# Batches 0 and 1 of a fused attention and swish-gate kernel in new orders on all engines

## Chip, cores and metric

The kernel runs on one core of one Trainium2 chip. The metric is the device time of one execution in microseconds (us). Most executions agree within 0.3%; for the comparisons below each kernel was run several times, in turn with the kernel before on the same chip. A profile is one execution with the hardware profiler; its span is about 1.8 us shorter than the device time. Times inside a profile count from the start of that span.

The engines are called TensorE (PE in the profile, PEld for its weight loads), VectorE (DVE), ScalarE (ACT), GpSimd (POOL) and the SyncE queue (SP), which issues the DMAs.

## The reference, cut to what matters

```python
# q, k, v: 8 batches x 8 heads x 576 x 64, float32
q_s = softmax(q, axis=-1); k_s = softmax(k, axis=2)
kv  = einsum('bhsd,bhse->bhde', k_s, v)
x   = einsum('bhsd,bhde->bhse', q_s, kv)      # -> 4608 tokens x 512
h   = x @ w_in                                # 512 x 2048
g   = h * sigmoid(beta * h)
out = g @ w_out                               # 2048 x 512
```

The main work is two large products, h and the output. One batch (512 of its 576 tokens; the tails form a ninth group) needs 16 h products of 4 matmuls and 16 output products of 4 matmuls, each matmul 128x128 by 128x512. Before the first h there is attention: exp(q), its sum and product, transposes, exp(k), kv, its norm, and x.

## The kernel before

The parts that the change touches (cuts are marked `# ...`):

```python
# exp(k) of batches 0 and 1: two heads share a tile, each in its own half of the
# partitions and of the columns; the other half is zero
def kz_exp(b, j, m=1):
    for e in range(2):
        r = slice(e * D, (e + 1) * D)
        nc.scalar.activation(ek[b][r, j : j + m, :, e * D : (e + 1) * D],
                             k_st[b][r, j : j + m, :].rearrange(...), ACTF.Exp)

def kv_mm(b, jj, n=2, tag="att"):             # batches 0 and 1: whole-array products
    # ...
    for i in range(RW):                       # RW = 9
        nc.tensor.matmul(t[:, jl, 0:D1], ek[b][:, j, i, :], va[b][:, j, i, :], ...)

# loads: q, k, v of batch 0, then w_in and w_out by turns
w_load("in", 0, 0); w_load("in", 0, 1); w_load("out", 0, 0); w_load("in", 1)
w_load("out", 0, 1); w_load("out", 1); w_load("in", 2); w_load("out", 2); w_load("in", 3)
# ... q, k, v of batch 1 among the last w_out

for p in range(HP):                           # batch 0: kv and x by head pair
    attn0(p)                                  # va cast, kv, norm
    # ...
    if p >= 1: x_mm(0, p - 1, nc.scalar)
    if p >= 2:
        for j in range(2): mm_a(0, j, [p - 2])   # first h, ahead of the last kv and x
# ...
for u in range(4, NJ):                        # then one h product, one output product
    mm_a(0, u); mm_b(0, u - LAG)              # ...
```

The softmax here doesn't subtract the row's maximum and nothing guards it: scores larger than these inputs give would overflow.

## Time and profile before

| | before |
|---|---|
| median of three runs | 288.42 us (288.05 to 288.63) |
| span of the profile | 286.1 us |
| TensorE busy | 278.1 us, 97% |
| first h matmul / dense stream of h and outputs | 16.08 us / 18.79 us |
| first output product of batch 1 | 52.61 us |

The first fence holds two lines of the page: busy time of each engine, and the shares of the chain of waits (the work that ended last, followed back through what released it).

```profile
PE 278.1 (97%) x1611; PEld 129.6 (45%) x1611; DVE 179.8 (63%) x281; ACT 162.7 (57%) x236; POOL 43.5 (15%) x58
...
PE 93%; DMA 4%; SPq 1%; POOL 0%; ACT 0%; DVE 0%; issue 0%
```

TensorE is the limit, and the chain runs over it nearly all the way. A matmul of 512 columns has a duration of 379 ns, but in a dense stretch the next one starts 0.216 us later; they overlap. So a busy share says little about gaps. The gaps in this document are taken from the starts: time from one start to the next, less 0.42 ns for each column (512 columns take 0.216 us in a dense stretch). A few matmul records are missing from the traces, and a gap of exactly 0.22 us is one of those.

The next fence is the timeline of the head: start, duration (from the first start to the last end of a merged run), engine, line, operation, out<-in, count, and in brackets the idle time before it and what ended it.

```profile
8.26 5.57 ACT L158 ACTIVATE ek<-k_st 64x576 bf16<-64x576 f32 x8 [1.16 <-DMA k_st<-in_k_dram]
...
14.98 1.04 POOL L145 CAST w_in_b<-w_in 128x1024 bf16<-128x1024 f32 x1 [0.81 <-DMA w_in<-in_moe_w_in_dram]
...
16.08 0.60 PE L358 MATMUL h<-xT,w_in_b 128*128 128x512 bf16 x2 [1.03 <-POOL w_in_b L145]
...
16.52 0.45 PE L264 MATMUL kv<-va,ek 128*128 128x65 bf16 x9
...
17.03 0.59 PE L358 MATMUL h<-xT,w_in_b 128*128 128x512 bf16 x2
...
17.73 0.39 PE L314 MATMUL x<-qsT,kvp 128*128 128x512 bf16 x1
...
17.96 0.59 PE L358 MATMUL h<-xT,w_in_b 128*128 128x512 bf16 x2
...
18.79 2.32 PE L358 MATMUL h<-xT,w_in_b 128*128 128x512 bf16 x10 [0.24 <-ACT xT L143]
```

The reader sees ScalarE making exp(k) in eight runs of 64 partitions, 0.68 us each; the first h waiting for its weights; and the last kv and x standing behind that h in TensorE's order. By 18.79 six h matmuls are done (the pairs at 16.08, 17.03 and 17.96; ten more follow, and the first four h products have sixteen), so the dense stream starts, in effect, at 18.79 - 6 x 0.216 = 17.49 us.

### The profile page before, as it was taken

To read this page: it belongs to the slowest core of one execution; us is meant where nothing else is said; L and a number is where in the kernel's file an instruction comes from. 1 tells how busy PE (TensorE), PEld (TensorE's weight loads), DVE (VectorE), ACT (ScalarE), POOL (GpSimd) and SP (SyncE) were. 2 spreads that over 40 slices of the span, in tenths; PEclk is the share of its full clock that TensorE was granted. 3 is DMA by queue.
4 is the path that set the end of the run, shared out by engine and by line. 5 is a ranking of instruction groups with operands and counts; after the bars stand their busy time and mean duration, and the time that the engine had idled before them with its cause. 6 is when DMAs were issued, how large, how long until landed. Compare 5 with 4: busy or idle time off the path is not lost.

```text
span 286.1 us, 4169 instructions
## 1 busy us (share of the span) xinstructions
PE 278.1 (97%) x1611; PEld 129.6 (45%) x1611; DVE 179.8 (63%) x281; ACT 162.7 (57%) x236; POOL 43.5 (15%) x58
## 2 busy tenths in 40 slices
PE   8789999999999999999999999999999999999995
PEld 2434445444444444444444444444445444445543
DVE  7935397695478456854694569546964596455361
ACT  4763596684486448735683468355934564554451
POOL 4358824200030021000300030002000000000000
PEclk9999999999999999999999999999999999999999
DMA  7999999908932973198219912794370033005003
GB/s 244 376 385 387 371 387 320 287 2 247 299 149 63 314 179 137 31 330 201 90 60 247 303 40 113 169 260 124 147 205 17 1 149 73 0 0 149 0 0 147
DMA packets 56371, 50.08 MB, mean 175 GB/s; under 512 B 26256, under 2 KB 48032, under 8 KB 56352
## 3 DMA queue, kind: packets, MB, share of 16 engines
q1 hardware_dynamic: 56208, 49.69, 56.5%
q8 instruction: 12, 0.20, 0.3%
q10 hardware_dynamic: 144, 0.13, 0.1%
q14 instruction: 7, 0.06, 0.1%
HBM read 36.71 MB, written 9.44 MB: 161 GB/s over the span
## 4 chain that ended last, share of the span: by engine, by line
PE 93%; DMA 4%; SPq 1%; POOL 0%; ACT 0%; DVE 0%; issue 0%
PE h L358 44%; PE acc L399 42%; DMA k_st<-in_k_dram 2%; PE x L314 2%; DMA w_in<-in_moe_w_in_dram 2%; PE kv L276 2%; PE acc L391 1%; PE kv L264 1%; PE tp L250 0%; POOL w_in_b L145 0%; SPq L85 0%; PE x L318 0%; ACT xT L143 0%; SPq L106 0%; DVE kvp L309 0%
## 5 line engine op out<-in xcount | busy, mean ns | idle before, releaser
L368 ACT ACTIVATE th<-h,beta_t 128x512 bf16<-128x512 f32 x144 | 98.5, 687 | 98.8 <-PE h L358 96.9
L370 DVE SCALAR_TENSOR_TENSOR g<-th,h 128x512 bf16<-128x512 bf16 x144 | 97.8, 681 | 88.8 <-ACT th L368 87.4
L358 PE MATMUL h<-xT,w_in_b 128*128 128x512 bf16 x576 | 145.3, 379 | 1.3 <-POOL w_in_b L145 1.0
L399 PE MATMUL acc<-w_out_b,g 128*128 128x512 bf16 x560 | 141.9, 379 | 0.0
L358 PEld LDWEIGHTS <-w_in_b 128*128 128x128 bf16 x576 | 55.4, 98 | 67.0 <-issue 2.7
L399 PEld LDWEIGHTS <-g 128*128 128x128 bf16 x560 | 54.5, 98 | 65.4 <-DVE g L370 0.5
L145 POOL CAST va<-v_st 128x2048 bf16<-128x2048 f32 (+2 forms) x12 | 16.9, 1414 | 146.6 <-DMA v_st<-in_v_dram 146.4
L225 DVE TENSOR_REDUCE rq<-eq 128x16 f32<-128x1024 bf16 x18 | 21.6, 1198 | 2.3 <-ACT eq L214 2.3
L231 DVE TENSOR_TENSOR eq<-eq,rq 128x1024 bf16<-128x1024 bf16 x18 | 22.1, 1229 | 0.1
L214 ACT ACTIVATE eq<-q_st 128x1024 bf16<-128x1024 f32 x16 | 16.3, 1047 | 3.0 <-DMA q_st<-in_q_dram 3.0
L143 ACT CAST xT<-x 128x512 bf16<-128x512 f32 x20 | 11.6, 586 | 10.8 <-PE x L314 10.0
L145 DVE COPY o<-acc 128x512 f32<-128x512 f32 (+1 forms) x19 | 12.1, 669 | 3.4 <-PE acc L399 3.2
L143 ACT COPY o<-acc 128x512 f32<-128x512 f32 (+1 forms) x18 | 9.5, 578 | 5.8 <-PE acc L399 2.9
L169 ACT ACTIVATE ek<-k_st 128x1024 bf16<-128x1024 f32 x12 | 12.6, 1047 | 0.0
L314 PE MATMUL x<-qsT,kvp 128*128 128x512 bf16 x32 | 11.7, 380 | 0.4 <-DVE kvp L309 0.2
L158 ACT ACTIVATE ek<-k_st 64x576 bf16<-64x576 f32 x16 | 10.9, 678 | 1.3 <-DMA k_st<-in_k_dram 1.2
L472 PE MATMUL warm<-kvp 128*128 128x512 bf16 x34 | 10.1, 439 | 1.2 <-DVE kvp L500 1.2
L145 DVE CAST xT<-x 128x512 bf16<-128x512 f32 x16 | 10.9, 683 | 0.5 <-PE x L314 0.5
L145 POOL CAST w_out_b<-w_out 128x1024 bf16<-128x1024 f32 x8 | 8.4, 1058 | 6.0 <-DMA w_out<-in_moe_w_out_dram 6.0
L309 DVE TENSOR_TENSOR kvp<-kv,rk 64x256 bf16<-64x256 f32 (+2 forms) x24 | 8.0, 334 | 0.6
L145 POOL CAST w_in_b<-w_in 128x1024 bf16<-128x1024 f32 x7 | 7.2, 1041 | 3.5 <-DMA w_in<-in_moe_w_in_dram 3.4
L472 PEld LDWEIGHTS <-kvp 128*128 128x128 bf16 x34 | 3.5, 109 | 5.4 <-issue 2.2
(40 smaller groups left out, 75.2 us busy)
## 6 DMA issues: line engine op xcount, KB each, us to landing
out_dram<-o SPq DMA_DIRECT2D x14, 512.0 KB, 3.4
q_st<-in_q_dram SPq DMA_DIRECT2D x6, 1024.0 KB, 6.4
k_st<-in_k_dram SPq DMA_DIRECT2D x6, 1024.0 KB, 9.4
v_st<-in_v_dram SPq DMA_DIRECT2D x6, 1024.0 KB, 10.7
w_in<-in_moe_w_in_dram SPq DMA_DIRECT2D x3, 1024.0 KB, 9.6
k_st<-in_k_dram SPq DMA_DIRECT2D x8, 288.0 KB, 8.1
q_st<-in_q_dram SPq DMA_DIRECT2D x4, 512.0 KB, 7.8
w_out<-in_moe_w_out_dram SPq DMA_DIRECT2D x4, 512.0 KB, 9.3
```

What stands on the lines that cost most here:

```text
L143: eng.copy(dst, src)
L145: eng.tensor_copy(dst, src)
L169: nc.scalar.activation(ek[b][:, :, h, :].rearrange("p i h d -> p h i d"), k_st[b][:, h, 0 : R * D].rearrange("p h (i d) -> p h i d", i=R), ...
L214: nc.scalar.activation(eq[b][:, :, s * m : (s + 1) * m, :].rearrange("p i h d -> p h i d"), q_st[b][:, s * m : (s + 1) * m, :].rearrange(" ...
L225: nc.vector.tensor_reduce(rq[b][:, 0, :, h], eq[b][:, :, h, :], axis=AX.X, op=ALU.add)
L231: nc.vector.tensor_tensor(eq[b][:, :, h, :], eq[b][:, :, h, :], rq[b][:, 1, :, h].unsqueeze(3).to_broadcast((P, R, m, D)), ALU.mult,)
L314: nc.tensor.matmul(t[:], kvp[:, c, j, :], qsT[c][:, :, j, :])
L358: nc.tensor.matmul(h[:], w_in_b[:, kt, ds(j * P, P)], x_of(c)[:, kt, :], start=(kt == 0), stop=(kt == KT - 1),)
L368: nc.scalar.activation(th[:], h[:], ACTF.Tanh, scale=beta_t[:, j : j + 1])
L370: nc.vector.scalar_tensor_tensor(out=g[:], in0=th[:], scalar=1.0, in1=h[:], op0=ALU.add, op1=ALU.mult)
L399: nc.tensor.matmul(acc[st][:], g[:, ds(st * P, P)], w_out_b[:, j, :], start=(j == 0), stop=(j == NJ - 1),)
L472: nc.tensor.matmul(t[:, 0:cols], kvp[:, B - 1, 0, :], kvp[:, B - 1, :, :].rearrange("p j r -> p (j r)")[:, 0:cols],)
```

## The change

The intent: have x ready when the first w_in piece arrives, run the first eight h products while w_out is still on its way, and give each engine an order of its own for batches 0 and 1. Everything from the fifth h product of batch 1 on is the same code, apart from the layout of the weights. The core of the diff (cut):

```diff
-        for e in range(2):                     # exp(k): dense, one activation per head pair
-            ... nc.scalar.activation(ek[b][r, j : j + m, :, e * D : (e + 1) * D], ...)
+        nc.scalar.activation(ek[b][:, j, :], k_st[b][:, j, :], ACTF.Exp)

+    def kvz_mm(b, j, tag="att"):               # kv in two quadrants of the array
+        for i in range(RW):
+            for e in range(2):
+                nc.tensor.matmul(att_of[b][r, j, 0:D1], ek[b][r, j, ds(i * D, D)], va[b][r, j, i, :],
+                                 ..., tile_position=(e * D, e * D))

-    w_out_d = moe_w_out.rearrange("(j p) f -> p j f", p=P)
+    w_out_d = moe_w_out.rearrange("(hh p e) f -> p hh e f", p=P, e=2)     # 4 KB runs, blocks 0, 1
+    w_out_4 = moe_w_out.rearrange("(blk p e) f -> p blk e f", p=P, e=4)   # 8 KB runs, blocks 2, 3

# so column q of an h product is every 2nd (blocks 0, 1) or every 4th column of w_in
+    w_in_u = [t[:].rearrange("p kt (q e) -> p kt e q", e=2) for t in w_in_b]
+            if blk >= EB:                      # blocks 2, 3: reordered by the cast
+                evac(eng, w_in_c[blk][:, c], t[:, c, :].rearrange("p kt (q e) -> p kt e q", e=4))

+    w_load("in", 0, 0)                         # all of w_in 0 and 1 ahead of w_out
+    ...beta_r, beta_q (behind w_in 0, 0)...
+    w_load("in", 0, 1); w_load("in", 1, 0); w_load("in", 1, 1)
+    w_load("out", 0, 0); w_load("out", 0, 1); w_load("in", 2); w_load("out", 1); w_load("in", 3)
+    ...
+    xpe(0, 2, "acc3"); ...; w_castk(0, 0, 1, G); beta_pe("acc1"); w_castk(0, 0, 0, A)
+    ...; xpe(0, 3, "acc2"); beta_ev()
+    hpe(0, 0, [0], "b0"); hpe(0, 1, [0], "b1"); ...      # h 0 to 7, then
+    mm_b(0, 0); mm_b(0, 1); mm_b(0, 2); mm_b(0, 3)       # outputs 0 to 3
+    hpe(0, 10, ...); hpe(0, 9, ...); hpe(0, 11, ...); hpe(0, 8, ...)
+    mm_b(0, 4) ... mm_b(0, 7); hpe(0, 12, ...) ... hpe(0, 15, ...); mm_b(0, 8) ...
+    # batch 1's kv in four groups (pairs 0, 3, 1, 2) among the outputs 9 to 14
```

## The prediction

> **What bounds it now.** TensorE: 97% busy on the page; the chain of waits puts 93% of the span on it. From 18.79 us its matmuls stand 0.216 us apart (timeline). So the time is the start of the dense h/output stream plus a fixed stream and tail. With four h matmuls already done, that start is effectively 18.79 - 0.86 = 17.9 us. Two things make it late (timeline): ScalarE runs eight 64-row exp(k) of 0.68 us, 8.26 to 13.83, before it evacuates any x; and TensorE, in order, takes the first h (16.08; its w_in landed at 14.93, GpSimd's cast took 1.04) ahead of the last kv/x pair, whose x is evacuated at 18.7. Second limit: DMA, 365 to 390 GB/s from 5 to 48 us; the last w_out lands at 41.4, batch 1's last v at 44.4.
>
> **What changes.**
> - Dense exp(k): four 128x576 activations for eight of 64x576; about 2.7 us less ScalarE per batch. The zero fills (1.98 us VectorE, 2.11 GpSimd) were off the path.
> - Loads: the same bytes precede the first w_in piece, so it should land at 14.9 again. Its cast is split over GpSimd and ScalarE (estimate 0.55 us). First h near 15.8, with x0 to x3 just ahead; w_in pieces at 1.47 us steps then feed h0 to h7 without w_out. Estimate: h6 ends at 22.7, minus 32 x 0.216 gives an effective start of 15.8: gain 2.1 us.
> - kv in quadrants: batches 2 to 7 already run pairs in about 32 ns, the full-array form takes 31: no gain. The Trainium skill (TensorEngine Tiling, Key Properties) says that a mode switch drains TensorE; this trace shows about 0.1 us at each edge of batch 2's group. Four groups in batch 1: about 0.8 us lost. Two warm matmuls fewer (0.43) and the small gaps pay that back.
> - Strided weights (every second w_in column for j below 8): the Trainium skill (TensorE: Matmul & The Clock Gate, weight-path perf modes) allows a column step in the fast load; loads take 98 ns under 216 ns matmuls.
> - w_out in 4 and 8 KB runs: 2 KB runs already reach about 387 GB/s; at most 0.3 us.
>
> **On the path.** By TensorE, batch 1's dense stream begins about 2.3 us earlier (effective 49.3 to 47.0). By DMA: loads end near 44.5 with the last w_out half, then cast 1.05, two output products 1.73, one x: about 47.1. The limits coincide, so slips add: w_in block 2 lands near 24.7, needed at 26.0; block 3 near 30, two strided GpSimd casts, needed at 33.0; w_out block 2 at 35.7, needed at 36.9. I allow 0.3 us. After batch 1's start the code is the same.
>
> **Predicted: 286.4 us** (8 in 10: 285.4 to 287.8). Faster by over 2%: 0.02; within 2%: 0.95; slower by over 2%: 0.03.
>
> **What would show it.** Right: first w_in still landing near 14.9, first h near 15.8, h6 ending near 22.7, batch 1's dense start 2 us earlier, the rest unchanged, 5 us less ScalarE in exp(k), kv pairs at about 32 ns. Wrong: first h after 16.5; TensorE gaps waiting for casts of w_in blocks 2, 3 or w_out 2, 3; DMA of batch 1 ending after 45.
>
> **What would make it wrong.** Strided weight loads that no longer hide (288 of them; 20 ns each would cost 5.8 us); strided GpSimd casts far above 1.04 us; lower GB/s with 1 KB runs; TensorE's clock dropping in an early gap.

## The result, and the profile after

| | before | after |
|---|---|---|
| median, first rounds | 288.40 us (4 runs) | 287.29 us (287.14 to 287.56, 4 runs) |
| ratio | | 0.9964, 95% interval 0.9947 to 0.9981 |
| median, repeated | 288.04 us (11 runs) | 287.59 us (286.94 to 287.88, 6 runs) |
| ratio, repeated | | 0.9978, 0.9964 to 0.9992 |
| span of the profile | 286.1 us | 285.8 us |
| first h / first output product | 16.08 / 20.95 us | 16.36 / 23.27 us |
| first output product of batch 1 | 52.61 us | 52.33 us |

A ratio is the mean time of one kernel's runs over that of the other's in the same rounds, so not quite the ratio of the medians. Executions over 1.5% slower than the fastest of the same kernel are left out of the means. By the medians the change gains 0.5 to 1.1 us, about a quarter to a half of the 2.0 us forecast. From the first output product of batch 1 to the end both profiles take the same (286.10 - 52.61 = 233.49, 285.78 - 52.33 = 233.45 us): all of the difference lies before it.

The same two lines of the page, after:

```profile
PE 277.2 (97%) x1655; PEld 130.2 (46%) x1684; DVE 178.0 (62%) x279; ACT 164.3 (57%) x238; POOL 42.9 (15%) x58
...
PE 85%; DMA 9%; DVE 1%; SPq 1%; ACT 1%; issue 1%; POOL 0%
```

The chain of this execution goes over DMA for 9% instead of 4%. Alone that proves little, as the share moves from trace to trace (2% and 12% for two versions below, 10% for one with the old order of loads). The timeline after, head first, then the two places where TensorE stops:

```profile
15.03 0.62 ACT L160 CAST w_in_b<-w_in 128x512 bf16<-128x512 f32 x1
15.06 0.62 POOL L162 CAST w_in_b<-w_in 128x512 bf16<-128x512 f32 x1 [0.82 <-DMA w_in<-in_moe_w_in_dram]
...
15.36 0.36 PE L577 MATMUL tb<-ident,beta_r 4*128 4x4 f32 x2
15.59 0.61 PE L579 MATMUL tb<-ident,beta_q 2*128 2x2 f32 x4
...
16.14 0.39 PE L370 MATMUL x<-qsT,kvp 128*128 128x512 bf16 x1
...
16.36 7.07 PE L420 MATMUL h<-xT,w_in_b 128*128 128x512 bf16 x31
...
25.26 2.06 ACT L160 CAST w_in_c<-w_in 128x1024 bf16<-128x1024 f32 x1 [0.44 <-DMA w_in<-in_moe_w_in_dram]
25.29 2.05 POOL L162 CAST w_in_c<-w_in 128x1024 bf16<-128x1024 f32 x1 [2.94 <-DMA w_in<-in_moe_w_in_dram]
...
27.39 3.63 PE L420 MATMUL h<-xT,w_in_c 128*128 128x512 bf16 x16 [0.51 <-POOL w_in_c L162]
...
30.60 4.04 POOL L162 CAST w_in_c<-w_in 128x1024 bf16<-128x1024 f32 x2 [1.68 <-DMA w_in<-in_moe_w_in_dram]
...
34.70 3.63 PE L420 MATMUL h<-xT,w_in_c 128*128 128x512 bf16 x16 [0.22 <-DVE rq L238]
```

Three things are to be seen. The h stream is dense from its first matmul, 16.36, against an effective 17.49 before: 1.13 us won. Both casts of w_in block 2 take 2.05 us where a cast of as many elements took 1.04 before, and the h of that block follows their end; the gap between matmul starts there is 0.67 us. Block 3's two casts take 4.04 us on GpSimd alone, end at 34.64, and the h follows at 34.70: the gap is 0.39 us. The profile names VectorE's `rq` as that releaser because it too ended just then; the h matmul reads nothing of it, so the cast is the one to take. The first h itself was ready to go earlier: its casts end at 15.68, but six tiny transposes of beta and the last x stand before it.

### The profile page after: what moved, and what is told of

It reads as the page before. It is cut to its first block, busy times and chain, and to the rows that moved or that the text cites. A ratio compares the mean times of both kernels' runs of the same rounds, so it can differ in the third digit from the quotient of the medians.

```text
span 285.8 us, 4292 instructions
## 1 busy us (share of the span) xinstructions
PE 277.2 (97%) x1655; PEld 130.2 (46%) x1684; DVE 178.0 (62%) x279; ACT 164.3 (57%) x238; POOL 42.9 (15%) x58
## 4 chain that ended last, share of the span: by engine, by line
PE 85%; DMA 9%; DVE 1%; SPq 1%; ACT 1%; issue 1%; POOL 0%
PE h L420 40%; PE acc L468 39%; DMA q_st<-in_q_dram 4%; DMA k_st<-in_k_dram 3%; DMA w_in<-in_moe_w_in_dram 3%; PE x L370 2%; PE kv L330 2%; PE acc L460 1%; SPq L115 1%; DVE g L434 1%; PE kv L289 1%; DVE rq L237 0%; POOL w_in_b L162 0%; ACT eq L226 0%; PE tp L274 0%
## 5 line engine op out<-in xcount | busy, mean ns | idle before, releaser
L468 PE MATMUL acc<-w_out_b,g 128*128 128x512 bf16 x547 | 138.9, 379 | 0.6 <-issue 0.2
L420 PE MATMUL h<-xT,w_in_c 128*128 128x512 bf16 x280 | 71.8, 379 | 1.1 <-POOL w_in_c L162 0.5
L420 PE MATMUL h<-xT,w_in_b 128*128 128x512 bf16 x281 | 70.9, 379 | 0.6
L420 PEld LDWEIGHTS <-w_in_b 128*128 128x128 bf16 x288 | 28.1, 98 | 33.9 <-issue 1.6
L420 PEld LDWEIGHTS <-w_in_c 128*128 128x128 bf16 x288 | 27.2, 98 | 32.6 <-POOL w_in_c L162 1.7
L162 POOL CAST va<-v_st 128x576 bf16<-128x576 f32 (+1 forms) x14 | 18.6, 1328 | 145.7 <-DMA v_st<-in_v_dram 145.6
L162 DVE CAST xT<-x 128x512 bf16<-128x512 f32 x19 | 13.0, 685 | 0.7 <-PE x L370 0.7
L162 POOL CAST w_in_c<-w_in 128x1024 bf16<-128x1024 f32 x3 | 6.1, 2047 | 4.6 <-DMA w_in<-in_moe_w_in_dram 4.6
L162 POOL CAST w_out_b<-w_out 128x1024 bf16<-128x1024 f32 x6 | 6.2, 1041 | 3.2 <-DMA w_out<-in_moe_w_out_dram 3.2
L174 ACT ACTIVATE ek<-k_st 128x576 bf16<-128x576 f32 x8 | 5.5, 681 | 2.0 <-DMA k_st<-in_k_dram 1.9
```

The source lines that it names most:

```text
L162: eng.tensor_copy(dst, src)
L420: nc.tensor.matmul(h[:], w_in_u[j // 2][:, kt, j % 2, :] if j < 4 * EB else w_in_c[j // 4][:, kt, j % 4, :], x_of(c)[:, kt, :], start=(kt ...
L468: nc.tensor.matmul(acc[st][:], g[:, ds(st * P, P)], w_out_b[:, j, :], start=(j == 0), stop=(j == NJ - 1),)
```

## Experiments

"The changed kernel" is the kernel after the change. The runs came in three groups of four (after_again to e12; e1b to e6; d1 to e17), each group on one chip with its own runs of the kernel before, so across groups the ratios are to be compared rather than the medians. The 95% intervals of a ratio are about +-0.0012 to 0.0023, that is 0.35 to 0.7 us. A trace is one execution and often not a typical one: those of e12 and e13 were the fastest of their six runs, those of e2, d1 and e17 the slowest.

### after_again: the changed kernel once more

> The changed kernel again, for a second trace and a tighter ratio. The two profiled runs differ by only 0.3 us in span (286.1 and 285.8), the medians by 1.1 us. If the trace pair tells the truth, the median gain is 0.3 to 0.6 us; if the profiled run of before was a lucky one, the gain stays near 1.1 us. In the trace I expect the same two TensorE stalls, 0.67 us near 27.4 us and 0.39 us near 34.7 us, and casts of w_in blocks 2 and 3 of 2.05 us each.

Measured: 287.59 us, ratio 0.9978 (0.9964 to 0.9992); span 285.9 us. The casts again took 2.02 to 2.05 us, and the stalls before blocks 2 and 3 were 0.87 and 0.40 us. But this trace has a third stall that the first has not:

```profile
17.59 1.17 POOL L162 CAST w_in_b<-w_in 128x512 bf16<-128x512 f32 x2 [2.44 <-DMA w_in<-in_moe_w_in_dram]
20.23 1.17 POOL L162 CAST w_in_b<-w_in 128x512 bf16<-128x512 f32 x2 [1.48 <-DMA w_in<-in_moe_w_in_dram]
...
21.46 1.90 PE L420 MATMUL h<-xT,w_in_b 128*128 128x512 bf16 x8 [0.51 <-POOL w_in_b L162]
```

The second half of w_in block 1 landed at 20.18 us, 2.65 us after the first half; in the first trace it was 19.53, 1.46 us after. TensorE loses 0.67 us by it, although the stream had started half a microsecond earlier (first h 15.83). It shows that the new order has put a load just ahead of its use, and that this load does not always keep its time. The two medians together put the gain at about 0.8 us.

### e1_dense_cast: casts in loaded order, weights read at a stride

```diff
-    w_in_c = {blk: const.tile([P, KT, 4, P], BF16, ...) ...}
+    w_in_c = {blk: const.tile([P, KT, 4 * P], BF16, ...) ...}
-                evac(eng, w_in_c[blk][:, c], t[:, c, :].rearrange("p kt (q e) -> p kt e q", e=4))
+                evac(eng, w_in_c[blk][:, c, :], t[:, c, :])
-                ... w_in_c[j // 4][:, kt, j % 4, :],
+                ... w_in_v[j // 4][:, kt, j % 4, :],   # w_in_v: the same tile as "p kt (q e) -> p kt e q", e=4
```

> One part undone: w_in blocks 2 and 3 are cast in the order in which they were loaded (dense reads), and TensorE reads every fourth column as weights. Theory A (the casts that read every fourth fp32 cost 2.05 us instead of 1.04 and hold up the first h products of both blocks): the casts fall to about 1.04 us on GpSimd and ScalarE, the stalls of 0.67 and 0.39 us vanish, and the time falls by about 1.0 us against the changed kernel. Rival B (these stalls only stand in front of a DMA limit): the casts get faster but the time comes back as waits for w_out block 2 or 3, and the total moves by less than 0.3 us. If weights read at a stride of four columns load slower than the matmuls hide, the steady part grows instead: 20 ns more on 288 loads would be 5.8 us.

Measured: 286.59 us against 287.59 for the changed kernel in the same rounds, ratio 0.9951 (0.9934 to 0.9968). The two fences show the view of the tile `w_in_c`, the changed kernel first: operation, count, shortest/median/longest duration in ns, first and last start.

```profile
L420 PEld LDWEIGHTS <-w_in_c x288: 95/98/99, 27.4 to 274.8; 128*128 128x128 bf16 x144
...
L162 POOL CAST w_in_c<-w_in x3: 2042/2047/2053, 25.3 to 32.6; 128x1024 bf16<-128x1024 f32 x3
L160 ACT CAST w_in_c<-w_in x1: 2058/2058/2058, 25.3 to 25.3; 128x1024 bf16<-128x1024 f32 x1
```

```profile
L421 PEld LDWEIGHTS <-w_in_c x288: 110/113/133, 26.0 to 274.1; 128*128 128x128 bf16 x144
...
L163 POOL CAST w_in_c<-w_in x3: 1040/1040/1041, 24.8 to 31.1; 128x1024 bf16<-128x1024 f32 x3
L161 ACT CAST w_in_c<-w_in x1: 1045/1045/1045, 24.8 to 24.8; 128x1024 bf16<-128x1024 f32 x1
```

The casts are down to 1.04 us on both engines and both stalls are gone. The weight loads pay 15 ns for reading every fourth column (113 against 98) and the matmuls stay at 379 ns and 0.216 us apart: no cost. The gain, 0.8 us by the ratios and 1.0 by the medians, is about what the two stalls were (1.06). Theory A holds: with the strided reads gone, so are the stalls. Not all came through: in this trace TensorE waits in a new place, before the output product of g 12, for w_out block 3 (landed 41.79, cast by 42.87, matmul at 42.93). Rival B is right about where the next limit lies. The size that it gave, under 0.3 us, is not what was measured, but it lies only at the edge of the noise (the means of the two sets of six runs differ by 0.8 +- 0.6 us).

### e1b_write_stride: the same reordering, with the stride on the write side

```diff
-                evac(eng, w_in_c[blk][:, c], t[:, c, :].rearrange("p kt (q e) -> p kt e q", e=4))
+                evac(eng, w_in_c[blk][:, c].rearrange("p kt e q -> p kt q e"),
+                     t[:, c, :].rearrange("p kt (q e) -> p kt q e", e=4))
```

> The changed kernel with the reordering casts of w_in blocks 2 and 3 turned round: they read in the loaded order and write every 128th bf16, and the result is the same. If it is the stride of the fp32 read (16 bytes) that doubles them to 2.05 us, they fall to about 1.04 us and the two stalls vanish as with the dense cast: about 1.0 us less than the changed kernel. If any reordering costs, whichever side is strided, they stay near 2 us and so does the time.

Measured: 293.44 us, ratio 1.0183 (1.0163 to 1.0202); both expectations missed. The timeline:

```profile
25.77 5.22 ACT L160 CAST w_in_c<-w_in 128x1024 bf16<-128x1024 f32 x1 [1.05 <-DMA w_in<-in_moe_w_in_dram]
25.80 5.22 POOL L162 CAST w_in_c<-w_in 128x1024 bf16<-128x1024 f32 x1 [2.94 <-DMA w_in<-in_moe_w_in_dram]
...
31.07 5.31 PE L420 MATMUL h<-xT,w_in_c 128*128 128x512 bf16 x16 [4.55 <-POOL w_in_c L162]
```

A dense read with a write that jumps 256 bytes per element costs 4.8 to 5.2 us on both engines, five times the dense cast. So it is not the read stride alone that costs; writing at a stride is worse. The run serves as a dose: a longer cast gives a longer stall (4.71 us before block 2, 1.50 before block 3), which is what Theory A says of these casts. The stall has a second price: the matmuls after it start 0.427 us apart instead of 0.216 until about 35 us. The Trainium skill (TensorE: Matmul & The Clock Gate, Part 1) says that TensorE falls to half its clock after an idle window of about 3.4 us; the trace agrees, with a stall of 4.71 us followed by a granted clock of 0.50 from 31.6 to 35.0 us.

### e2_beta_early and e12_both: beta out of the way

```diff
+    nc.scalar.dma_start(beta_r[:], ...)        # first of all loads, on ScalarE's queue
+    nc.scalar.dma_start(beta_q[:], ...)
     load_q(0, 2, 0)
...
     warm(4, tag="acc1")
+    beta_pe("acc1"); beta_ev()                 # was between x 2 and x 3
     kvz_mm(0, 0, "acc2")
```

> One part moved: the two small beta loads go first, on ScalarE's queue, and beta's six transposes run before the first kv products, where TensorE idles 1.35 us. Theory A: the first h comes about 0.5 us earlier (near 15.85 instead of 16.36), but the total does not move (under 0.2 us), because the cast of w_in block 2, which follows its load at 25.2 us, still ends near 27.3 us and the stall there grows by the 0.5 us. Rival C (the late first h is the whole shortfall against the prediction): the total falls by 0.5 us.

> Both edits. Theory A: they add, about 1.5 us less than the changed kernel (1.0 from the casts and 0.5 from beta, which now counts as no stall absorbs it). Rival B: the last half of w_out block 3, which lands near 44.8 us and is cast by 45.9 us, becomes the limit: under this theory the sum is below 1.2 us and TensorE waits before the output product of g 14.

Measured: beta early alone 287.74 us, ratio 0.9985 (0.9969 to 1.0000); on top of the dense casts 286.90 us, ratio 0.9956 (0.9940 to 0.9972). Neither gains on its base. As a move it half worked: the first h came 0.91 and 1.11 us after the landing of its w_in piece, against 1.35 in both traces of the changed kernel. But e1's and e13's traces, with beta where it was, have 1.20 and 1.22, so the move itself brings less than these figures suggest. In the trace of e2 the first q piece landed at 5.13 us instead of 4.59, and the first w_in piece at 15.21 (14.89 in e12's), against 15.01 and 14.48 in the changed kernel's traces. That loading beta first delays the q piece is not shown: in e1's trace, without that edit, it landed at 5.13 too. In the trace of e2 the second half of w_in block 1 landed 3.02 us after the first, and TensorE stood 1.21 us there, then 0.92 and 0.63 before blocks 2 and 3. The early h of 15.85 was not reached (16.12, in the slowest of e2's runs), so these runs do not decide between Theory A and Rival C: the total stayed, as A said, but the cause that it was to withstand was hardly applied. For e12, A's sum of 1.5 us was missed (0.7), and so was Rival B's wait before g 14: in e12's trace the cast of that half ends at 45.71 and the matmul starts at 45.92. There the loads of w_in block 1 came on time, and from the first h to batch 1 TensorE has no gap beyond those of the mode changes; that execution took 286.25 us.

### e13_fewer_switches and e15_full_kv_batch1: the array-mode changes of batch 1

In the traces of the changed kernel each of batch 1's four kv groups has about 0.10 us of gap before and after it: the Trainium skill (TensorEngine Tiling, Key Properties) says that a change of tiling mode drains TensorE, and the measured price is 0.10 us an edge, 0.8 us for eight. Two ways of having fewer, both on the dense-cast version:

```diff
# e13: two groups instead of four
-    kvz_mm(1, 0, "b1") ... kvz_mm(1, 3) ... kvz_mm(1, 1) ... kvz_mm(1, 2)
+    kvz_mm(1, 0, "b1"); kvz_mm(1, 3) ... kvz_mm(1, 1); kvz_mm(1, 2)   # x 0 and x 1 moved behind the next output product
# e15: batch 1 as in the kernel before
+        if b == 1:   # zero-filled ek, two 64-row exp(k), 9 whole-array matmuls a pair
```

> The dense-cast version with batch 1's four groups of kv products joined into two, so four changes between whole-array and quarter-array matmuls instead of eight, each about 0.10 us in the traces. If these edges are on the path, 0.4 us less than the dense-cast version. If the arrival of w_out block 3 limits that stretch (its first half made TensorE wait 0.5 us, 0.74 with the edge's rest, before the output product of g 12 in the dense-cast trace), less than 0.2 us.

> The dense-cast version with batch 1's kv made as in the kernel before: 64-row exp(k) into a zero-filled tile and 36 whole-array products; batch 0 keeps the quadrants. No array-mode change is left in batch 1, so 0.8 us less TensorE time than with quadrants; ScalarE gets 2.7 us more to do there. If the mode changes are a loss on the path: about 0.8 us less than the dense-cast version, unless w_out block 3's arrival caps it at about 0.3. If ScalarE's extra exps hold up kv: no gain or a loss.

Measured: e13 286.69 us, ratio 0.9944 (0.9925 to 0.9962); e15 287.24 us, ratio 0.9967 (0.9943 to 0.9990). Against the dense-cast version (0.9951) neither is a gain that these intervals can show. In e13's trace four edges are gone as meant, but TensorE waits 0.26 us before the output product of g 12, for w_out block 3 (cast 40.41 to 41.45, matmul at 41.50), and 0.33 us between two x. In e15's trace the waits between 36 and 50 us are these (engine, what it waited for, total us, times, longest):

```profile
PEld L302 <- ACT ek L182: 1.8, 4, 0.6
DVE qsT L163 <- ACT qsT L161: 1.7, 1, 1.7
...
PE x L393 <- DVE qsT L163: 0.6, 1, 0.6
```

Here the two-part exp(k) (1.37 us a pair instead of 0.68) makes ScalarE late: kv waits for it, then the transposed q, and x stands for a gap of 0.77 us. (That trace also has a late w_in block 1, 0.70 us.) So in this trace other waits fill the 0.8 us of TensorE time that e15 saves. That the dense exp(k) more than pays for its mode changes in batch 1 is not shown: e15 and the dense-cast version cannot be told apart.

### e6_dense_exp_only: one part of the change on the kernel before

```diff
 # on the kernel before: kz_exp dense, kv_mm in quadrants, no zero fills; orders and loads as before
```

> One part of the change alone on the kernel before: dense exp(k), kv in quadrants, no zero fills, everything else as before. My theory: the head does not get shorter, because the first h waits for the w_in piece (landing 14.93) and its 1.04 us cast, and the last kv and x stand behind it in TensorE's order; the first h stays near 16.1 us and the array-mode changes of two groups of batch 1 cost 0.4 us, so between unchanged and 0.5 us slower than before. Rival: ScalarE's exp(k) chain, 8.26 to 13.83, holds up the head; then the dense form gains 0.5 us or more.

Measured: 288.53 us, ratio 1.0010 (0.9996 to 1.0025): no gain, as my theory had it. ScalarE's timeline shows why:

```profile
14.11 0.59 ACT L143 CAST xT<-x 128x512 bf16<-128x512 f32 x1 [4.21 <-PE x L310]
```

With exp(k) done early, ScalarE idles 4.21 us and evacuates the first x at 14.11; in the kernel before it was 14.10. The chain of exp(k), which I had named first among the causes of the late start, did not hold up the first x. The rest of the trace was not as expected: the first h came at 15.12 and not near 16.1, because its w_in piece landed at 13.77 (14.93 before), and the dense stream, again with six h matmuls done, at 17.95 instead of 18.79. The total did not fall with it: TensorE then waited 0.38 us for an h at 37.83 and 1.11 us (0.25 before) for VectorE's q before the transposes at 39.79. By batch 1's h after the last x it was behind (49.82 us, 49.05 before), four mode changes included. So here too a head that was 0.84 us early gained nothing at the end. The 1.13 us of the change's head come, by exclusion, from the orders and the loads, which use the room that the dense form gives; how much of it each of them brings was not separated.

### d1_delay_after and d2_delay_e1: TensorE made busy on purpose

```diff
+    warm(3, tag="b3")            # three dummy matmuls, 0.65 us
     hpe(0, 0, [0], "b0")
```

> The changed kernel with three dummy matmuls (0.65 us of TensorE) right before the first h of batch 0. Theory A: the head's gain is partly idle, because the h products of w_in blocks 2 and 3 wait for casts whose ends do not depend on TensorE; so the stall near 27.4 us shrinks by what the dummies take, and the time grows by less than 0.3 us. Rival: the start of the h stream sets the time, then it grows by 0.65 us.

> The same three dummies in the dense-cast version, where those stalls are gone. Theory A: nothing absorbs them up to w_out block 3, so 0.3 to 0.65 us more than the dense-cast version's 286.6 us, about 287.1. If its time does not grow either, the limit there is the arrival of data.

Measured: d1 287.70 us, ratio 0.9994 (0.9975 to 1.0012), against 0.9978 for the changed kernel: 0.1 us by the medians, 0.5 by the ratios, which is inconclusive. Its profiled run (289.07) was the slowest one, with the second q piece at 9.39 us instead of 8.21, and is no guide. d2 286.87 us, ratio 0.9953 (0.9941 to 0.9966) against 0.9951: nothing to 0.3 us. The two traces of the dense-cast version, without and with the dummies, the piece around g 12:

```profile
41.84 1.04 POOL L163 CAST w_out_b<-w_out 128x1024 bf16<-128x1024 f32 x1 [1.34 <-DMA w_out<-in_moe_w_out_dram]
...
42.93 1.02 PE L469 MATMUL acc<-w_out_b,g 128*128 128x512 bf16 x4 [0.57 <-POOL w_out_b L163]
```

```profile
41.70 1.04 POOL L163 CAST w_out_b<-w_out 128x1024 bf16<-128x1024 f32 x1 [0.17 <-DMA w_out<-in_moe_w_out_dram]
...
42.93 1.03 PE L469 MATMUL acc<-w_out_b,g 128*128 128x512 bf16 x4
```

The h stream started 0.59 us later with the dummies (16.48 against 15.89), and both traces arrive at g 12's output at 42.93: the first waits there for w_out, the second has no wait left. In this pair the arrival of data took up the whole delay. An earlier start of the stream is worth nothing there.

### e16_best and e17_no_wout3: the parts together, and with less to load

e16 is e13 with beta's loads on ScalarE's queue after the first exp(k) and its transposes before the first kv; e17 is e16 with the loads of w_out block 3 left out and block 2's data cast in their place. Its output is wrong, which doesn't matter for the time.

> Dense casts, kv groups of batch 1 joined, and beta's loads on ScalarE's queue after the first exp(k) (near 6 us, since loading them first delayed the first q piece by 0.5 us), its transposes before the first kv. Expected: first h 0.9 to 1.1 us after the landing of the first w_in piece instead of 1.2 to 1.35, TensorE work 0.4 us shorter in batch 1; 0.3 to 0.8 us less than the dense-cast version if TensorE limits, no gain if data arrival does.

> Wrong on purpose: the version before with 1 MB less to load, block 3 of w_out made from block 2's data. If the arrival of the last loads of batches 0 and 1 limits that version, 0.4 us or more less than it, and no TensorE wait before the output product of g 12; if TensorE limits it, under 0.2 us.

Measured: e16 286.73 us, ratio 0.9959 (0.9937 to 0.9980), correct; e17 286.97 us, ratio 0.9961 (0.9943 to 0.9978), relative error 0.70 as intended. Neither expectation of a gain was met. In e16's trace the first h came 1.21 us after its piece landed (0.9 to 1.1 expected), and the piece after it was late (17.06, 2.35 us after the first): TensorE stood 0.33 us at 17.75 and 0.45 us at 21.88 for w_in. e17's trace has no wait before g 12 any more, so that wait was indeed w_out block 3. Its median does not fall, which by the expectation speaks against the last loads as the limit; the intervals of the two ratios (0.5 and 0.6 us each way) do not exclude the gain. The traced execution, the slowest of the six, had another late load, w_in block 1:

```profile
21.58 1.17 POOL L163 CAST w_in_b<-w_in 128x512 bf16<-128x512 f32 x2 [1.85 <-DMA w_in<-in_moe_w_in_dram]
...
22.81 1.90 PE L421 MATMUL h<-xT,w_in_b 128*128 128x512 bf16 x7 [1.27 <-POOL w_in_b L163]
```

Over ten traces of these kernels in which both landings can be read, the second half of w_in block 1 came 1.46 or 1.47 us after the first in six (after, e1, e1b, e12, e13, d1) and 2.65 to 3.02 us after it in four (after_again, e2, e15, d2). Of the 1 KB packets between 12 and 24 us, the last ended 1.4 to 2.4 us after 98% of them were through in the late traces, 0.6 to 1.1 us in the others, and came one at a time, as if one of the 16 DMA engines were behind. In all of them an instruction fetch, one packet of 16 KB, holds a DMA engine for 1.0 to 1.15 us, starting between 17.8 and 20.7 us. Whether that fetch is what delays the piece was not tested; it stays open.

The version that beats both kernels by the least edit is the dense-cast one, 286.59 us. What was added to it (beta, fewer mode changes, both) gave 286.7 to 286.9 and cannot be told from it.

## Why the prediction was right or wrong

The time, 287.3 us and 287.6 when repeated, lies in the range that was given (285.4 to 287.8), and "within 2%" was right. The range was wide enough to hold a good part of the miss: its slow end is 0.2 us above the repeat. Of the signs named for a wrong prediction one appeared, the gaps waiting for casts of w_in blocks 2 and 3. The gain was about half or less of the 2.0 us forecast. Term by term, from the pair of profiles (us; minus is a gain):

| term | predicted | measured |
|---|---|---|
| effective start of the h stream | -2.1 (17.9 to 15.8) | -1.13 (17.49 to 16.36) |
| slips: casts of w_in blocks 2 and 3 | +0.3 (all slips) | +0.67 + 0.39 = +1.06 |
| array-mode changes of batch 1 | +0.8 | +0.8 (8 x 0.10) |
| two warm matmuls fewer, small gaps | -1.0 | -1.01 (what is left over) |
| sum at the start of batch 1's outputs | -2.0 | -0.28 (52.61 to 52.33) |

That pair of executions is a little unkind to the change: by the medians it gains 1.1 and 0.5 us. The profiled run of before, 287.87, was faster than all of its first four timed runs (288.05 to 288.63), and the profiled run of after, 287.56, was the slowest of its four.

- "With four h matmuls already done" is a miscount: six were done. The start to be improved on was 17.49 and not 17.9, so a first h that led to an effective 15.8 would have gained 1.7 us and not 2.1. Put right, the same sum forecasts about 1.6 us, or 286.8 us (an estimate from that count). The rest of the head's shortfall, 0.56 us, is the later first h in this pair of traces.
- "Block 3 near 30, two strided GpSimd casts, needed at 33.0" and "block 2 lands near 24.7, needed at 26.0" are the terms that were mis-sized most. I counted 1.04 us for a cast, which I had measured on dense reads, and named strided casts "far above 1.04 us" only as a risk. They took 2.05 us each, on ScalarE as well as on GpSimd. Block 2 also landed later than forecast, at 25.24, but a cast of 1.04 us would have ended at 26.30, before TensorE came to it at 26.72. e1_dense_cast shows that this was worth 0.8 to 1.0 us, most of the distance from 286.4 to the measured time. The Trainium skill had the warning: the GPSIMD Engine Reference, section 7, gives about 50% more for reads with a step over 8 bytes (in its own kernels on that engine), and SBUF — State Buffer, section "Door 1: The DMA port swizzle", tells of 16-byte lines that need two hits to run at full rate. With a step of 16 bytes each line is hit once.
- "First h near 15.8 with x0 to x3 just ahead" held only in part. In the profile it was 16.36, and 15.83 in the repeat, where the piece landed at 14.48. Measured from the landing it was 1.35 us both times, not the 0.9 predicted. I had overlooked that beta's loads moved behind the w_in piece, so its six transposes and the last x now follow the piece as well. That they are the whole delay is not shown: with beta early it was 0.91 (e2), 1.11 (e12) and 1.21 us (e16). The arrivals behind this term absorb a later start (d2, in its pair of traces); whether an earlier one would reach the end, e2 does not settle.
- "w_in pieces at 1.47 us steps then feed h0 to h7 without w_out" held in the first profile and in five other traces of ten; in the remaining four the fourth piece came 1.2 to 1.6 us late, and the margin of about half a microsecond was too thin.
- "The limits coincide, so slips add" was the right frame, and 0.3 us for it was too little.
- Right: 0.8 us for the mode changes; the kv pairs at about 32 ns (a group of 18 matmuls takes 0.48 us, as 0.45 before for nine whole-array ones); no cost of strided weights (98 ns at a step of two, and 113 at four in e1, both hidden under 216 ns, so the skill's statement about the column step of the fast load agrees with the trace as far as no cost shows); the last load of batch 1 at 44.81 us (44.5 predicted); the rest of the kernel unchanged.
- Wrong without effect: exp(k) was named first among the causes of the late head; in e6 the dense form alone gains nothing that an interval of +-0.4 us can show.

## What to carry to other kernels

When a kernel's loads and its busiest engine reach the same point within a few tenths of a microsecond, moving the engine's work earlier gains only what the arrivals allow; write down for every piece when it lands, what its cast takes and when it is needed, and give it at least the spread seen between executions. Measure a cast in the access pattern in which it will run: here a reorder in the cast doubled (read side) or quintupled it (write side), while the same reorder in the weight load was free. And test a suspected bottleneck by taking it away alone, because the exp(k) chain that looked like the cause of the late start gained nothing when it alone was shortened.

## What the Trainium skill lacked or had wrong

- SBUF — State Buffer, section "Door 1: The DMA port swizzle", says that one can stride for free up to 4 fp32, and in the same note that a line of 16 bytes needs at least two hits. A read of every fourth fp32 (one hit per line) was not free: 2.05 us against 1.04 for 128x1024 elements, on ScalarE and GpSimd alike. The two-hit rule agrees; the "4 fp32", read as a step of four, does not.
- GPSIMD Engine Reference, section 7, gives +50% for a step over 8 bytes; the cast on GpSimd took +97% at 16 bytes. It tells of reads only: a write of bf16 at a step of 256 bytes took 4.8 to 5.2 us on both engines, and none of the pages that I read has a figure for that.
- TensorEngine Tiling, Key Properties, says that a mode switch drains TensorE without a figure: 0.10 us of gap per edge here.
- TensorE: Matmul & The Clock Gate, weight-path perf modes, allows strided columns in the fast load but gives no times for them: 98 ns at a step of one and two, 113 ns at four, for 128x128 bf16.
- None of the pages that I read tells how far the landing of one load varies between executions of the same program: the same 512 KB piece came 1.46 us after its predecessor in six traces and 2.65 to 3.02 us in four.
